# An adaLN attention block on one core: the output projection, residual and first norm of the last 512 tokens rearranged

## The chip, the core and the metric

The kernel runs on one core of a Trainium2 chip. The metric is the device time of one execution in microseconds (us); three runs of the kernel before gave 826.66, 824.58 and 827.45, median 826.66. The engines are TensorE (PE, with its weight loads as PEld), VectorE (DVE), ScalarE (ACT), GpSimd (POOL) and SyncE (SP), which issues most DMAs. Matrix products go to PSUM, eight banks of 128 x 512 float32; DVE and ACT read them there, POOL does not.

## What is computed

One transformer block with conditioning, for 2048 tokens of 512 features, 32 heads of 16, and a hidden layer of 1376:

```python
mod = (silu(c) @ w_mod).reshape(1, 6, 1, 512)      # sa, ca, ga, sb, cb, gb
h = layernorm(x) * (1 + ca) + sa
q, k, v = heads(h @ wqkv)
x = x + ga * (softmax(q @ k.T * 16 ** -0.5) @ v) @ wo
h = layernorm(x) * (1 + cb) + sb
x = x + gb * (gelu(h @ w1 + b1) @ w2 + b2)
```

## The kernel before

**Attention.** The 2048 queries are 4 blocks of 512 tokens, the 32 heads 8 groups of 4. A block and a group make a "quad"; there are 32 quads, each with 16 key tiles of 128. For a quad, PE computes the scores of 4 heads (row-tiled products, L941), and either ACT takes their exponential (L993, three or two rows at a time: `pA`, `pB`) or, for up to four key tiles of a quad, DVE makes it with integer operations (L1059, L1080: the "D" tiles). PE then adds the products with the values into one PSUM bank, `od` (L1136). An extra column of ones gives the sum of the weights in the same bank. When a quad is complete, DVE copies `od` to `o_sb` (L1168), the sums travel by DMA through DRAM and back (L1171, L1172, L1185, L1187, L1189), and POOL divides (L1193, tile `OT`). Only the last quad does this on the spot: shuffle, reciprocal and product on DVE from `o_sb` (L1177 to L1179).

**The tails.** When the 8 quads of a block are done, its tail follows: output projection (8 products for each 128 tokens), the gate `ga` (DVE, L584), the residual (POOL, L587), the statistics of the norm (DVE, L196), norm, transposes, modulation, the up projection with GELU, the down projection (L643, L645), gate `gb` and residual (L651, L655). The tails of blocks 0 to 2 run in between the attention of the next block.

**What sets the order.** A planner in the kernel's Python (`pe_step`, `dve_step`, ... and the list `jobs`) keeps a clock for each engine with costs such as `MM = 0.215` or `V_EVAC = 0.63`, and writes out each engine's instructions in the order in which its clocks allow them. A job has a due time in quads (`p0 + 0.5` is half a quad after the block's last), a list of rows (engine, cost, function), labels that it needs, and, where it needs PSUM, one of two banks `aux`, which it shares with the D tiles. `hold` tells after which row the bank is free again. Where PE has too little to do, the planner adds products with zeros (L1157). The engines themselves work strictly in the order that was written.

**The last tail** is not planned. When the last quad is complete, the pools of the attention are closed (`att.close()`), and `last_tail` writes its instructions one after the other: a pool of 8 PSUM banks `fb` on the space of the closed pools; 32 products of the output projection, quad by quad over four token tiles (L687); `norm_half(0)` for the first two token tiles: gate (L694), residual (L696), statistics on DVE; eight small operations for mean and root; the norm (L227); the eight transposes of the half (L232), read out by DVE (L272) and ACT (L269), each into a bank of its own; `norm_half(1)` with the residual on POOL (L699); the up projection of each half (L719) with GELU on ACT (L721), the down projection of four token tiles (L726, L728), gate and residual on DVE (L731, L733) and the store (L734). Between the halves' up projections stand the transposes of the second half; `range_flag` checks the sums (L753 to L761, L744, L745) for a general path that is not taken here.

Of the kernel before, what the change touches and what calls it, by code (L numbers as in the profile page):

```python
# [11 lines left out]
ALU = mybir.AluOpType  # L12
# [43 lines left out]
PE_LAT = 0.18  # L56
EXP = {1: 0.5, 2: 0.92, 3: 1.34}

EARLY = 0.95
# [28 lines left out]
def adaln_block(ctx: ExitStack, tc: tile.TileContext, A_x, A_wqkv, A_wo, B_x, B_w1, B_b1, B_w2, B_b2,  # L88
# [320 lines left out]
    def job(at, rows, needs=(), label=None, hold=-1):  # L409
        jobs.append(Job(at, rows, needs, label, hold))  # L410
# [87 lines left out]

    job(4.5, [(DVE_, 2.2, load_wo)], (), "wo")

# [55 lines left out]
    def tail_jobs(b):  # L556
# [15 lines left out]
        def oproj(tt):  # L572
            def f(part):
                def g(j):
                    if part == 0:
                        j.ps = j.alloc()
                    for t in (2 * part, 2 * part + 1):
                        nc.tensor.matmul(out=j.ps, lhsT=OT[(b, t)][:, tt * P:(tt + 1) * P], rhs=W_o_pad[:, t, :],  # L578
                                         start=(t == 0), stop=(t == 7))
                return g  # L580

            def mul(j):
                j.tmp = late["tl2"].tile([P, D], FP32, name="tmp")
                nc.vector.tensor_tensor(out=j.tmp, in0=j.ps, in1=ga_b, op=ALU.mult)  # L584

            def res(j):
                nc.gpsimd.tensor_tensor(out=T["x1"][:, tt, :], in0=j.tmp, in1=T["xr"][:, tt, :], op=ALU.add)  # L587

            def stats(j):
                ln_stats(T["x1"], T["st"], tt, tt)  # L590
            job(p0 + 0.5 + 0.25 * tt, [(PE_, 2 * MM, f(i)) for i in range(4)]
                + [(DVE_, V_EVAC, mul), (POOL_, 1.2, res), (DVE_, V_EVAC, stats)],
                ["wo", ("begin", b)] + [("ot", b, t) for t in range(8)] + ([("o", b, tt - 2)] if tt > 1 else []),
                ("o", b, tt), 4)
# [69 lines left out]
    for b in range(NQB - 1):  # L664
        tail_jobs(b)
    jobs.sort(key=lambda o: o.at)

    def last_tail():
# [3 lines left out]
        W_1, W_2, b1c = late["W_1"], late["W_2"], late["b1c"]  # L672
        xr = tl.tile([P, 4, D], BF16, name="xr")
        nc.sync.dma_start(out=xr, in_=x_tok[b])
        x1 = xr
        h2 = tl.tile([P, NC, 512], BF16, name="h2T")
# [3 lines left out]
        st = tl.tile([P, 4, 6], FP32, name="st2")  # L680
        with tc.tile_pool(name="fps", bufs=8, space=PSUM) as fps:
            def bank(dt=FP32, n=512):
                return fps.tile([P, n], dt, name="fb")
            po = [bank() for _ in range(4)]
            for t in range(8):
                for tt in range(4):
                    nc.tensor.matmul(out=po[tt], lhsT=OT[(b, t)][:, tt * P:(tt + 1) * P], rhs=W_o_pad[:, t, :],  # L687
                                     start=(t == 0), stop=(t == 7))
            def norm_half(hf):
                tts = (2 * hf, 2 * hf + 1)  # L690
                tmps = []
                for tt in tts:
                    tmp = tl2.tile([P, D], FP32, name="tmp")
                    nc.vector.tensor_tensor(out=tmp, in0=po[tt], in1=ga_b, op=ALU.mult)  # L694
                    if hf == 0:
                        nc.vector.tensor_tensor(out=x1[:, tt, :], in0=tmp, in1=xr[:, tt, :], op=ALU.add)  # L696
                        ln_stats(x1, st, tt, tt)
                    else:
                        nc.gpsimd.tensor_tensor(out=x1[:, tt, :], in0=tmp, in1=xr[:, tt, :], op=ALU.add)  # L699
                if hf:  # L700
                    for tt in tts:
                        ln_stats(x1, st, tt, tt)
# [20 lines left out]

            def down_tile(tt):
                ps = bank()
                nc.tensor.matmul(out=ps, lhsT=ones_row, rhs=late["b2r"], start=True, stop=False)  # L726
                for fc in range(NFC):
                    nc.tensor.matmul(out=ps, lhsT=uG[:, fc, tt * P:(tt + 1) * P], rhs=W_2[:, fc, :],  # L728
                                     start=False, stop=(fc == NFC - 1))
                tmp = tl2.tile([P, D], FP32, name="tmp")  # L730
                nc.vector.tensor_tensor(out=tmp, in0=ps, in1=gb_b, op=ALU.mult)  # L731
                o = tl2.tile([P, D], BF16, name="ob")
                nc.vector.tensor_tensor(out=o, in0=tmp, in1=x1[:, tt, :], op=ALU.add)  # L733
                nc.sync.dma_start(out=out_tok[4 * b + tt], in_=o)  # L734
# [40 lines left out]
    def general_tile(g, gp):  # L775
        W_1, W_2, b1c = late["W_1"], late["W_2"], late["b1c"]
        tok = bass.ds(g * P, P)
        with tc.tile_pool(name="gw", bufs=1) as gw, tc.tile_pool(name="gs", bufs=1, space=PSUM) as gs, \
# [54 lines left out]
            tmp = gw.tile([P, D], FP32, name="gtmp")  # L833
            nc.vector.tensor_tensor(out=tmp, in0=ps, in1=ga_b, op=ALU.mult)
            nc.vector.tensor_tensor(out=x1[:, 0, :], in0=tmp, in1=x1[:, 0, :], op=ALU.add)
            st = gw.tile([P, 1, 6], FP32, name="gst")
# [327 lines left out]
    def do_out(qi):  # L1164

        b, t = quads[qi]
        o = odp.tile([P, 512], FP32, name="o_sb")
        nc.vector.tensor_copy(out=o, in_=od[qi])  # L1168
# [4 lines left out]
        if qi == nq - 1:  # L1173
            rb = odp.tile([P, 512], FP32, name="rb")
            ot = otp.tile([P, 512], BF16, name="OT")
            OT[(b, t)] = ot
            nc.vector.stream_shuffle(out=rb, in_=o, mask=[16] * 32)  # L1177
            nc.vector.reciprocal(out=rb, in_=rb)
            nc.vector.tensor_tensor(out=ot, in0=o, in1=rb, op=ALU.mult)  # L1179
            return  # L1180
# [175 lines left out]
    while pv["q"] < nq or od_copy or jobs or active:  # L1356
        q = next_quad[0] - 1
        act_prog[0] = max(0.0, next_quad[0] - (len(stream) + len(unit["next"] or ())) / (4.0 * (NKT - len(d_of(q)))))
        moved = False
# [7 lines left out]
    att.close()  # L1367
    last_tail()
    general_path()

# [34 lines left out]
```

## Time and profile before

| what | value |
|---|---|
| the profiled execution's own time | 827.04 us |
| its span | 825.3 us |
| the three runs shown | 824.58 to 827.45 us, median 826.66 |
| busy share of the span | PE 94%, ACT 91%, DVE 89%, POOL 9% |
| last product of the attention issued | at about 779.1 us of the span |
| last output product ended | at about 819.9 us |
| last DVE operation ended | at about 821.3 us |
| ACT idle ahead of its exponentials, all quads | 10.3 + 11.3 us |
| filling products (L1157) | 920 into `od`, 32 into `aux` |

The profile is one execution on the chip. Times are microseconds from the start of the span; a timeline line gives start, duration (of a group of equal instructions, the whole stretch), engine, line of the kernel, operation, written and read tiles, shapes and count, and in brackets how long the engine stood idle ahead of it and what ended that. Products are pipelined: one of 128 x 512 shows 0.38 to 0.39 us, but the next follows after 0.216 us. PEclk is the share of the full clock that TensorE was granted.

### The profile page before, as it was taken

What the parts mean: (1) busy time and instruction counts of PE and PEld (TensorE: products, weight loads), DVE (VectorE), ACT (ScalarE), POOL (GpSimd) and SP (SyncE); (2) the same over time, 40 slices, a digit from 0 to 9 for tenths busy, and PEclk for the clock granted to TensorE, in tenths of its full rate; (3) what the DMA queues carried; (4) which work ended last, traced back from release to release, by engine and by line L of the source; (5) the groups of instructions that cost most, each with busy time, mean ns of one, the idle gap of its engine ahead of it and who ended that gap; (6) DMA issues with size and microseconds to landing.
All of it is one profiled execution on the core that took longest, in us unless ns stands there. A gap on an engine that the chain in (4) does not pass through costs nothing.

```text
span 825.3 us, 18246 instructions
## 1 busy us (share of the span) xinstructions
PE 774.9 (94%) x7438; PEld 239.6 (29%) x7503; DVE 732.9 (89%) x1323; ACT 750.4 (91%) x670; POOL 75.2 (9%) x68
## 2 busy tenths in 40 slices
PE   7999999999999999999999999998999999999967
PEld 3332222223222222222223222222223222222343
DVE  6858999999999899989989999989988999988573
ACT  2899799999999999999989999999999999999732
POOL 0000010010011000011021000011012000111010
PEclk8999999999999999999999999999999999999979
DMA  9000000104100000000100000100100000010000
GB/s 306 27 1 15 7 24 23 23 23 142 41 16 14 15 16 15 22 15 23 41 14 17 15 16 15 22 13 22 41 16 15 16 16 12 12 28 22 20 22 28
DMA packets 29626, 24.49 MB, mean 30 GB/s; under 512 B 13825, under 2 KB 23394, under 8 KB 29538
## 3 DMA queue, kind: packets, MB, share of 16 engines
q1 hardware_dynamic: 28482, 22.23, 9.6%
q8 instruction: 60, 0.98, 0.5%
q10 hardware_dynamic: 1056, 1.05, 0.4%
q14 instruction: 28, 0.23, 0.1%
HBM read 20.65 MB, written 2.61 MB: 28 GB/s over the span
## 4 chain that ended last, share of the span: by engine, by line
PE 42%; ACT 30%; DVE 16%; issue 10%; DMA 2%; SPq 0%; POOL 0%; ACTq 0%; DVEq 0%; POOLq 0%
ACT pA L993 16%; PE od L1136 12%; ACT pB L993 11%; DVE t L1059 6%; PE sA L941 6%; DVE t L1080 5%; PE sB L941 5%; PE aux L645 3%; PE aux L941 3%; PE aux L578 2%; ACT uG L634 2%; PE fb L719 1%; PE od L1157 1%; PE aux L620 1%; PE fb L728 1%
## 5 line engine op out<-in xcount | busy, mean ns | idle before, releaser
L993 ACT ACTIVATE pA<-sA 128x1536 bf16<-128x1536 f32 x310 | 469.3, 1514 | 10.3 <-PE od L1136 5.4
L1059 DVE TENSOR_SCALAR t<-aux 128x512 int16<-128x512 f32 x500 | 327.8, 679 | 29.2 <-PE aux L941 27.5
L993 ACT ACTIVATE pB<-sB 128x1024 bf16<-128x1024 f32 x309 | 337.0, 1091 | 11.3 <-PE od L1136 6.1
L1080 DVE TENSOR_SCALAR t<-t 128x2048 int16<-128x2048 int16 x375 | 262.8, 722 | 2.1 <-PE od L1136 0.5
L941 PE MATMUL aux<-qm,kT 32*128 32x512 bf16 x500 | 176.3, 379 | 3.3 <-DVE t L1059 1.6
L941 PEld LDWEIGHTS <-kT 32*128 32x128 bf16 x2048 | 77.6, 91 | 268.6 <-issue 263.7
L1136 PE MATMUL od<-pA,VE 128*32 128x512 bf16 x930 | 143.5, 385 | 0.4 <-DVE o_sb L1168 0.4
L1136 PE MATMUL od<-pB,VE 128*32 128x512 bf16 x618 | 142.5, 385 | 0.0
L1136 PE MATMUL od<-t,VV 128*32 128x512 f16 x1500 | 137.8, 384 | 1.6 <-DVE t L1080 1.5
L941 PE MATMUL sA<-qm,kT 32*128 32x512 bf16 x930 | 123.2, 383 | 14.4 <-ACT pA L993 9.6
L941 PE MATMUL sB<-qm,kT 32*128 32x512 bf16 x618 | 121.2, 383 | 5.8 <-ACT pB L993 2.1
L1193 POOL TENSOR_TENSOR OT<-o_sb,rb 128x512 bf16<-128x512 f32 x31 | 41.6, 1342 | 530.0 <-DMA rb<-d 363.2
L1157 PE MATMUL od<-hT,zeros 128*32 128x512 bf16 x920 | 80.8, 383 | 0.0
L1136 PEld LDWEIGHTS <-VE 128*32 128x32 bf16 x2048 | 50.1, 94 | 99.3 <-issue 86.5
L1136 PEld LDWEIGHTS <-VV 128*32 128x32 bf16 x1500 | 40.0, 95 | 55.9 <-issue 46.5
L1136 PE MATMUL od<-t,VE 128*32 128x512 f16 x500 | 49.2, 384 | 0.9 <-DVE o_sb L1168 0.9
L620 PE MATMUL aux<-h2T,W 128*128 128x512 bf16 x114 | 36.0, 385 | 0.8 <-DVE t L1059 0.7
L645 PE MATMUL aux<-W,uG 128*128 128x512 bf16 x119 | 34.9, 383 | 1.8 <-issue 1.7
L1157 PEld LDWEIGHTS <-zeros 128*32 128x32 bf16 x952 | 23.3, 95 | 36.4 <-issue 29.2
L1168 DVE COPY o_sb<-od 128x512 f32<-128x512 f32 x32 | 21.8, 682 | 8.7 <-issue 8.5
L625 DVE TENSOR_SCALAR uG<-aux,b1c 128x512 bf16<-128x512 f32 x33 | 24.3, 737 | 2.7 <-PE aux L620 2.6
L578 PE MATMUL aux<-W_o_pad,OT 128*128 128x512 bf16 x88 | 24.7, 383 | 0.3 <-issue 0.3
(129 smaller groups left out, 418.4 us busy)
## 6 DMA issues: line engine op xcount, KB each, us to landing
rb<-d SPq DMA_DIRECT2D x124, 64.0 KB
W_m<-in_w_mod_dram SPq DMA_DIRECT2D x2, 1024.0 KB
xr<-in_A_x_dram SPq DMA_DIRECT2D x4, 512.0 KB
out_dram<-ob SPq DMA_DIRECT2D x16, 128.0 KB
xb<-in_A_x_dram SPq DMA_DIRECT2D x3, 512.0 KB
W<-in_B_w_dram SPq DMA_DIRECT2D x1, 1376.0 KB
W<-in_B_w_dram SPq DMA_DIRECT2D x1, 1280.0 KB
W_m<-in_w_mod_dram ACTq DMA_DIRECT2D x1, 1024.0 KB
```

What stands on the lines that cost most here:

```text
L578: nc.tensor.matmul(out=j.ps, lhsT=OT[(b, t)][:, tt * P:(tt + 1) * P], rhs=W_o_pad[:, t, :], start=(t == 0), stop=(t == 7))
L620: nc.tensor.matmul(out=j.ps, lhsT=late["W_1"][:, c, fc * P:(fc + 1) * P], rhs=T["h2"][:, c, :], start=(c == 0), stop=(c == NC - 1))
L625: nc.vector.tensor_scalar(out=T["u"][:, fc, :], in0=j.ps, scalar1=late["b1c"][:, fc:fc + 1], scalar2=None, op0=ALU.add)
L645: nc.tensor.matmul(out=j.ps, lhsT=T["u"][:, fc, tt * P:(tt + 1) * P], rhs=late["W_2"][:, fc, :], start=False, stop=(fc == NFC - 1))
L941: nc.tensor.matmul(out=dst, lhsT=kT[32 * r:32 * r + 32, ch, kt * P:(kt + 1) * P], rhs=qm[(b, ch)][32 * r:32 * r + 32, par, :], start=True, ...
L993: nc.scalar.activation(out=pt[:, 0:n, :], in_=st[:, 0:n, :], func=ACT.Exp, scale=math.log(2.0) / STEP)
L1059: nc.vector.tensor_scalar(out=t0[(qi, kt)][:, r, :], in0=sd, scalar1=T_BIAS, scalar2=0.0, op0=ALU.add, op1=ALU.max)
L1080: nc.vector.tensor_scalar(out=t16, in0=t0[(qi, kt)], scalar1=float(MJ[j]), scalar2=None, op0=ALU.add)
L1136: nc.tensor.matmul(out=od[qi][32 * r:32 * r + 32, :], lhsT=w, rhs=src, start=first, stop=last_)
L1157: nc.tensor.matmul(out=dst[32 * r:32 * r + 32, :], lhsT=zeros, rhs=hT[:, r, 0:512], start=bank is not None, stop=bank is not None)
L1168: nc.vector.tensor_copy(out=o, in_=od[qi])
L1193: nc.gpsimd.tensor_tensor(out=OT[(b, t)], in0=o, in1=j.rb, op=ALU.mult)
```

## The change

The gate `ga` is multiplied once into the output weights (`scale_wo`: eight POOL products of 128 x 512, planned at quads 6 to 7.4). The residual comes into PSUM as one more product, of the identity with the tokens `xr`, ahead of the eight of each token tile; in the tails of blocks 0 to 2 a DVE copy then takes the place of gate and POOL residual. The due times of the down projection's four tiles are 0.6 quads apart, formerly 0.5.

For the last block, the load of its tokens (`last_begin`) and the projections of token tiles 0 and 1 without the last quad's part are planned jobs in the last quad, in the two `aux` banks, which now belong to a pool that stays open. `last_tail` has six PSUM banks on the space of the attention's closed pools. It writes the seven quads' products of tiles 2 and 3, five products that are not used (`keep_on`), the last quad's four products, and eighteen more unused ones. The statistics are read from PSUM by DVE, the sums copied to SBUF by ACT. A one-column GELU stands ahead of the first transposes. Two transposed chunks share one PSUM bank. The down projection of tile 0 stands ahead of the second half's transposes, and that of tile 3 is done in two halves of 256 columns. The last quad's shuffle and product read `od` itself, and the copy `o_sb` comes after them.

```diff
+KEEP = (5, 18)
...
+    def scale_wo(t):
+        nc.gpsimd.tensor_tensor(out=W_o_pad[:, t, :], in0=W_o_pad[:, t, :], in1=ga_b, op=ALU.mult)
...
+    bk = ExitStack()
+    banks = [bk.enter_context(tc.tile_pool(name=f"psX{i}", bufs=1, space=PSUM)) for i in range(2)]
     att = ExitStack()
...
-    banks = [att.enter_context(tc.tile_pool(name=f"psX{i}", bufs=1, space=PSUM)) for i in range(2)]
...
-    job(4.5, [(DVE_, 2.2, load_wo)], (), "wo")
+    job(4.5, [(DVE_, 2.2, load_wo)], (), "wo_in")
+    for t in range(8):
+        job(6.0 + 0.2 * t, [(POOL_, 1.2, lambda j, t=t: scale_wo(t))], ["wo_in", "ga"], ("wo", t))
...
+                        nc.tensor.matmul(out=j.ps, lhsT=ident, rhs=T["xr"][:, tt, :], start=True, stop=False)
...
-            def mul(j):
-                j.tmp = late["tl2"].tile([P, D], FP32, name="tmp")
-                nc.vector.tensor_tensor(out=j.tmp, in0=j.ps, in1=ga_b, op=ALU.mult)
-
             def res(j):
-                nc.gpsimd.tensor_tensor(out=T["x1"][:, tt, :], in0=j.tmp, in1=T["xr"][:, tt, :], op=ALU.add)
+                nc.vector.tensor_copy(out=T["x1"][:, tt, :], in_=j.ps)
...
-            job(p0 + 4.9 + 0.5 * tt, [(PE_, (3 if i == 0 else 1 if i == 5 else 2) * MM, f(i)) for i in range(6)]
+            job(p0 + 4.9 + 0.6 * tt, [(PE_, (3 if i == 0 else 1 if i == 5 else 2) * MM, f(i)) for i in range(6)]
...
+    def last_begin(j):
+        last["xr"] = late["tl"].tile([P, 4, D], BF16, name="xr")
+        nc.sync.dma_start(out=last["xr"], in_=x_tok[NQB - 1])
+
+    job(8 * NQB - 1.2, [(SP_, 3.0, last_begin)], [("tail", NQB - 2)], "last")
+
+    def o_mm(ps, tt, t):
+
+        if t == 0:
+            nc.tensor.matmul(out=ps, lhsT=ident, rhs=last["xr"][:, tt, :], start=True, stop=False)
+        nc.tensor.matmul(out=ps, lhsT=OT[(NQB - 1, t)][:, tt * P:(tt + 1) * P], rhs=W_o_pad[:, t, :],
+                         start=False, stop=(t == 7))
+
+    def last_oproj(tt):
...
+        job(8 * NQB - 1.0 + 0.05 * tt, [(PE_, n * MM, f(i)) for i, n in enumerate((3, 2, 2, 1))],
+            ["last", "d_done"] + [("ot", NQB - 1, t) for t in range(7)], ("last", tt), 99)
...
-        with tc.tile_pool(name="fps", bufs=8, space=PSUM) as fps:
+        with tc.tile_pool(name="fps", bufs=6, space=PSUM) as fps:
...
-            po = [bank() for _ in range(4)]
-            for t in range(8):
-                for tt in range(4):
-                    nc.tensor.matmul(out=po[tt], lhsT=OT[(b, t)][:, tt * P:(tt + 1) * P], rhs=W_o_pad[:, t, :],
-                                     start=(t == 0), stop=(t == 7))
+            po = [last[0], last[1], bank(), bank()]
+            for tt in (2, 3):
+                for t in range(7):
+                    o_mm(po[tt], tt, t)
+
+
+            idle = bank()
+
+            def keep_on(n):
+                for _ in range(n):
+                    nc.tensor.matmul(out=idle, lhsT=ident, rhs=hT[:, 0, 0:512], start=True, stop=True)
+            keep_on(KEEP[0])
+            for tt in range(4):
+                o_mm(po[tt], tt, 7)
+            keep_on(KEEP[1])
...
+                    nc.vector.bn_stats(out=st[:, tt, :], in_=po[tt])
+                    nc.scalar.copy(out=x1[:, tt, :], in_=po[tt])
...
-                    pst = bank(BF16, 256)
+                    if j % 2 == 0:
+                        two = bank(BF16, 512)
+                    pst = two[:, 256 * (j % 2):256 * (j % 2) + 256]
...
             norm_half(0)
+
+            early = tl.tile([P, 1], FP32, name="early")
+            nc.scalar.activation(out=early, in_=b1c[:, 0:1], func=ACT.Gelu_apprx_tanh)
             transposes(0)
             norm_half(1)
             up_half(0)
+            down_tile(0)
             transposes(1)
             up_half(1)
...
-            for tt in range(4):
+            for tt in (1, 2):
                 down_tile(tt)
+            down_tile(3, 2)
...
+        if qi == nq - 1:
+            rb = odp.tile([P, 512], FP32, name="rb")
+            nc.vector.stream_shuffle(out=rb, in_=od[qi], mask=[16] * 32)
+            nc.vector.reciprocal(out=rb, in_=rb)
+            ot = otp.tile([P, 512], BF16, name="OT")
+            OT[(b, t)] = ot
+            nc.vector.tensor_tensor(out=ot, in0=od[qi], in1=rb, op=ALU.mult)
         o = odp.tile([P, 512], FP32, name="o_sb")
         nc.vector.tensor_copy(out=o, in_=od[qi])
...
         if qi == nq - 1:
-            rb = odp.tile([P, 512], FP32, name="rb")
-            ot = otp.tile([P, 512], BF16, name="OT")
-            OT[(b, t)] = ot
-            nc.vector.stream_shuffle(out=rb, in_=o, mask=[16] * 32)
-            nc.vector.reciprocal(out=rb, in_=rb)
-            nc.vector.tensor_tensor(out=ot, in0=o, in1=rb, op=ALU.mult)
             return
```

More of the change, by code (lines that the diff above doesn't have):

```diff
@@ L576, in g @@
                         j.ps = j.alloc()
+                        nc.tensor.matmul(out=j.ps, lhsT=ident, rhs=T["xr"][:, tt, :], start=True, stop=False)
                     for t in (2 * part, 2 * part + 1):
                         nc.tensor.matmul(out=j.ps, lhsT=OT[(b, t)][:, tt * P:(tt + 1) * P], rhs=W_o_pad[:, t, :],
-                                         start=(t == 0), stop=(t == 7))
+                                         start=False, stop=(t == 7))
                 return g
-            def mul(j):
-                j.tmp = late["tl2"].tile([P, D], FP32, name="tmp")
-                nc.vector.tensor_tensor(out=j.tmp, in0=j.ps, in1=ga_b, op=ALU.mult)
             def res(j):
-                nc.gpsimd.tensor_tensor(out=T["x1"][:, tt, :], in0=j.tmp, in1=T["xr"][:, tt, :], op=ALU.add)
+                nc.vector.tensor_copy(out=T["x1"][:, tt, :], in_=j.ps)
             def stats(j):
                 ln_stats(T["x1"], T["st"], tt, tt)
-            job(p0 + 0.5 + 0.25 * tt, [(PE_, 2 * MM, f(i)) for i in range(4)]
-                + [(DVE_, V_EVAC, mul), (POOL_, 1.2, res), (DVE_, V_EVAC, stats)],
-                ["wo", ("begin", b)] + [("ot", b, t) for t in range(8)] + ([("o", b, tt - 2)] if tt > 1 else []),
+            job(p0 + 0.5 + 0.25 * tt, [(PE_, (2 + (i == 0)) * MM, f(i)) for i in range(4)]
+                + [(DVE_, V_EVAC, res), (DVE_, V_EVAC, stats)],
+                [("begin", b)] + [("wo", t) for t in range(8)] + [("ot", b, t) for t in range(8)] + ([("o", b, tt - 2)] if tt > 1 else []),
                 ("o", b, tt), 4)
@@ L665, in adaln_block, with f, g @@
         tail_jobs(b)
+    last = {}
+    def last_begin(j):
[6 more added lines that the diff above has]
+        nc.tensor.matmul(out=ps, lhsT=OT[(NQB - 1, t)][:, tt * P:(tt + 1) * P], rhs=W_o_pad[:, t, :],
+                         start=False, stop=(t == 7))
+    def last_oproj(tt):
+        def f(part):
+            def g(j):
+                if part == 0:
+                    j.ps = last[tt] = j.alloc()
+                for t in range(2 * part, min(7, 2 * part + 2)):
+                    o_mm(j.ps, tt, t)
+            return g
+        job(8 * NQB - 1.0 + 0.05 * tt, [(PE_, n * MM, f(i)) for i, n in enumerate((3, 2, 2, 1))],
+            ["last", "d_done"] + [("ot", NQB - 1, t) for t in range(7)], ("last", tt), 99)
+    for tt in range(2):
+        last_oproj(tt)
     jobs.sort(key=lambda o: o.at)
@@ L672, in last_tail @@
         W_1, W_2, b1c = late["W_1"], late["W_2"], late["b1c"]
-        xr = tl.tile([P, 4, D], BF16, name="xr")
-        nc.sync.dma_start(out=xr, in_=x_tok[b])
-        x1 = xr
+        x1 = last["xr"]
         h2 = tl.tile([P, NC, 512], BF16, name="h2T")
@@ L680, in last_tail @@
         st = tl.tile([P, 4, 6], FP32, name="st2")
-        with tc.tile_pool(name="fps", bufs=8, space=PSUM) as fps:
+        with tc.tile_pool(name="fps", bufs=6, space=PSUM) as fps:
             def bank(dt=FP32, n=512):
                 return fps.tile([P, n], dt, name="fb")
-            po = [bank() for _ in range(4)]
-            for t in range(8):
-                for tt in range(4):
-                    nc.tensor.matmul(out=po[tt], lhsT=OT[(b, t)][:, tt * P:(tt + 1) * P], rhs=W_o_pad[:, t, :],
-                                     start=(t == 0), stop=(t == 7))
+            po = [last[0], last[1], bank(), bank()]
[10 more added lines that the diff above has]
+            keep_on(KEEP[1])
             def norm_half(hf):
                 tts = (2 * hf, 2 * hf + 1)
-                tmps = []
                 for tt in tts:
[L693 to L702, printed above, removed]
+                    nc.vector.bn_stats(out=st[:, tt, :], in_=po[tt])
+                    nc.scalar.copy(out=x1[:, tt, :], in_=po[tt])
                 mv, rs = ln_rstd(st[:, 2 * hf:2 * hf + 2, :], 2)
@@ L722, in up_half, with down_tile @@
                                          bias=b1c[:, fc:fc + 1], scale=1.0)
[L724 to L729, printed above, removed]
-                tmp = tl2.tile([P, D], FP32, name="tmp")
[L731 to L734, printed above, removed]
+            def down_tile(tt, parts=1):
+                o = tl2.tile([P, D], BF16, name="ob")
+                tmp = tl2.tile([P, D], FP32, name="tmp")
+                n = D // parts
+                for c in range(parts):
+                    cs = slice(c * n, c * n + n)
+                    ps = bank(FP32, n)
+                    nc.tensor.matmul(out=ps, lhsT=ones_row, rhs=late["b2r"][:, cs], start=True, stop=False)
+                    for fc in range(NFC):
+                        nc.tensor.matmul(out=ps, lhsT=uG[:, fc, tt * P:(tt + 1) * P], rhs=W_2[:, fc, cs],
+                                         start=False, stop=(fc == NFC - 1))
+                    nc.vector.tensor_tensor(out=tmp[:, cs], in0=ps, in1=gb_b[:, cs], op=ALU.mult)
+                    nc.vector.tensor_tensor(out=o[:, cs], in0=tmp[:, cs], in1=x1[:, tt, cs], op=ALU.add)
+                    nc.sync.dma_start(out=out_tok[4 * b + tt][:, cs], in_=o[:, cs])
             norm_half(0)
+            early = tl.tile([P, 1], FP32, name="early")
+            nc.scalar.activation(out=early, in_=b1c[:, 0:1], func=ACT.Gelu_apprx_tanh)
             transposes(0)
@@ L833, in general_tile @@
             tmp = gw.tile([P, D], FP32, name="gtmp")
-            nc.vector.tensor_tensor(out=tmp, in0=ps, in1=ga_b, op=ALU.mult)
-            nc.vector.tensor_tensor(out=x1[:, 0, :], in0=tmp, in1=x1[:, 0, :], op=ALU.add)
+            nc.vector.tensor_tensor(out=x1[:, 0, :], in0=ps, in1=x1[:, 0, :], op=ALU.add)
             st = gw.tile([P, 1, 6], FP32, name="gst")
@@ L1357, in adaln_block @@
         q = next_quad[0] - 1
+        if not d_tiles and not d_items:
+            lab.setdefault("d_done", clock)
         act_prog[0] = max(0.0, next_quad[0] - (len(stream) + len(unit["next"] or ())) / (4.0 * (NKT - len(d_of(q)))))
@@ L1368, in adaln_block @@
     last_tail()
+    bk.close()
     general_path()
```

## Prediction

> **What bounds the kernel now.** I read the page's busy shares first (PE 94%, ACT 91%, DVE 89%), then the groups by line, the waits, and the timeline from 777 us. Up to 779 us PE and ACT keep each other at work; ACT waits ahead of its exponentials only 10.3 + 11.3 us in all:
>
> ```profile
> L993 ACT ACTIVATE pA<-sA 128x1536 bf16<-128x1536 f32 x310 | 469.3, 1514 | 10.3 <-PE od L1136 5.4
> L993 ACT ACTIVATE pB<-sB 128x1024 bf16<-128x1024 f32 x309 | 337.0, 1091 | 11.3 <-PE od L1136 6.1
> DVE st L196 <- POOL xr L587: 3.6, 4, 1.3
> ```
>
> The third line (waits) is all that the residual on POOL costs DVE. After 779 us a chain alternates between DVE and PE (timeline: start, duration, engine, line, tiles, in brackets the idle time before and what ended it):
>
> ```profile
> 779.56 0.69 DVE L1168 COPY o_sb<-od 128x512 f32<-128x512 f32 x1 [8.55 <-issue]
> 780.30 0.72 DVE L1177 STREAM_SHUFFLE rb<-o_sb 128x512 f32<-128x512 f32 x1
> 780.40 7.07 PE L687 MATMUL fb<-W_o_pad,OT 128*128 128x512 bf16 x31 [0.72 <-DVE o_sb L1168]
> 781.05 3.35 DVE L1178 RECIPROCAL rb<-rb 128x512 f32<-128x512 f32 x1
> 784.44 0.69 DVE L1179 TENSOR_TENSOR OT<-o_sb,rb 128x512 bf16<-128x512 f32 x1
> 786.93 0.69 DVE L694 TENSOR_TENSOR tmp<-fb,ga_b 128x512 f32<-128x512 f32 x1 [1.79 <-PE fb L687]
> 793.20 0.73 DVE L227 TENSOR_SCALAR hnL<-xr,mv,rs 128x512 bf16<-128x512 bf16 x2
> 793.67 1.25 PE L232 MATMUL fb<-ident,hnL 128*128 128x128 bf16 x8 [6.20 <-DVE hnL L227]
> ```
>
> Two things are to be seen. PE stands idle for 6.2 us before the transposes. And the first output product waits for the copy `o_sb`, though it reads nothing of it: the new pool lies on the space of the closed ones and waits for their last reader. The rows of windows (length, busy PE, PEld, DVE, ACT, POOL, granted clock) show the price of the idle time:
>
> ```profile
> 787.00:788.00 1.00, 0.47 (x3) 0.00 (x0) 0.91 (x2) 0.00 (x0) 0.00 (x0) 1.00 0.00 0
> 789.00:790.00 1.00, 0.00 (x0) 0.00 (x0) 0.97 (x3) 0.00 (x0) 0.00 (x0) 0.87 0.00 0
> 790.00:791.00 1.00, 0.00 (x0) 0.00 (x0) 0.97 (x2) 0.00 (x0) 0.00 (x0) 0.50 0.00 0
> 799.00:800.00 1.00, 1.00 (x7) 0.71 (x5) 0.83 (x6) 0.57 (x2) 0.00 (x0) 0.51 0.00 0
> 800.00:801.00 1.00, 1.00 (x11) 0.89 (x10) 0.82 (x6) 0.77 (x2) 0.00 (x0) 1.00 0.00 0
> ```
>
> PE stopped at 787.47, the clock fell at about 789.7 and came back at 800.0, 6.3 us after work began again at 793.67. Both steps are 10.3 us apart.
>
> **Quads 0 to 30.** Removed: 12 gate products and 12 POOL sums; added: 12 copies (0.68 each, from `o_sb`'s group), 12 identity products (12 x 0.216 = 2.6 us of PE) and 8 POOL products of some 1.3 us in quads 6 and 7, where POOL has 90% free; if they came late, the first output projection, in quad 8, would wait. The changed program's order has 900 filling products where before had 952, so most of the 2.6 us replaces filling. At best the 3.6 us of DVE's wait and part of ACT's idle time go; at worst 12 + 16 products add 28 x 0.216 = 6 us less 52 fillings of about 0.065 (16 in 1.04 us), 3.4: about +2.6. I take -0.7, near the gain's lower half, since DVE seldom ends ACT's waits; the range keeps -3.6 to +2.6. The token load goes from SP's free stretch at 782 us to just after the sums of quad 30 go out, ahead of the store of their reciprocals (764.4). That quad's `OT` was ready at 772.3 (POOL, 770.99 + 1.27) and would be wanted by the planned products near 776: 3.7 us of slack, beyond which PE's scores queue behind them. The two planned projections sit in the two `aux` banks after the last D tile. Cost nothing while that slack holds.
>
> **The wait that moves.** In the changed program's order the copy `o_sb` is last of DVE's four operations, and PE's first product of tile 2 (7 + identity, then tile 3) still waits for it. So the chain is: shuffle 779.56, reciprocal 780.31, product 783.70 (each 0.74 earlier, the copy being gone), copy 784.42 to 785.11, PE at 785.26 (0.15 after the copy, as before). PE is idle 779.47 to 785.26, 5.8 us. The planned start would have been near 779.5: the 16 products that were to fill this gap stand behind it.
>
> First statistics: 16 + 5 products x 0.2155 = 4.53, start of the last quad's first at 789.79, 0.50 until DVE can read (before: product 28 x 0.2155 after 780.40, DVE at 786.93): 790.29 warm. After an idle time of 5.8 us the clock is low: the idle stretch of before sufficed after 2.3 us. Low for 3.4 to 6.8 us of work (6.3 in the row above, and half of that at best if a step falls well), half of it lost: 1.7 to 3.4; I take 2.4. So 792.65, against 786.93. From there the old chain to `hnL` took 6.27; four of its operations (2 gate, 2 residual, 2.85 by the starts) are gone: 3.42, `hnL` 796.07. Three forms have no row yet: shuffle, product and statistics that read PSUM. Their rows from SBUF are 0.72, 0.69 and 0.69, DVE's copy and gate from PSUM take 0.69 each, so I take them as unchanged; at twice the statistics' price it would be 1.4 more, at none 1.4 less. The sums' copies by ACT (0.55 for 256 columns, 1.09 for 1024, so some 0.7) wait for the statistics of their tile in the same bank and end near 794.7, ahead of `hnL`: hidden, and beyond 796.07 each microsecond would count. PE is held by the 18 products: 785.26 + 43 x 0.2155 + 2.4 = 796.93, transposes there instead of 793.67: **+3.26**.
>
> [...]
>
> **Transposes.** Two chunks share a bank, so each second chunk's transposes wait for the reading of the first, and DVE and ACT alternate. By the rows below (0.41 each on DVE, 0.55 on ACT, 0.3 to 0.4 from PE to reader) full rate comes 2.55 after the first transpose, where it was 1.98: up projection at 799.5 against 795.65, **+3.85**. The table load (1.28) goes into ACT's idle time before the transposes, where it costs nothing; it did not bind before either.
>
> ```profile
> 794.32 0.83 DVE L272 TENSOR_SCALAR h2T<-fb,modc 128x256 bf16<-128x256 bf16 x2 [0.39 <-PE fb L232]
> 794.58 1.02 ACT L269 ACTIVATE h2T<-fb,modc 128x256 bf16<-128x256 bf16 x2 [15.57 <-PE fb L232]
> ...
> 796.09 1.28 ACT L721 ACT_TABLE_LOAD   x1 [0.49 <-issue]
> ...
> 802.53 1.37 DVE L272 TENSOR_SCALAR h2T<-fb,modc 128x256 bf16<-128x256 bf16 x4 [0.88 <-PE fb L232]
> ...
> 804.26 4.84 ACT L721 ACTIVATE uG<-fb,b1c 128x256 bf16<-128x256 f32 x11 [1.37 <-PE fb L719]
> 819.91 0.69 DVE L731 TENSOR_TENSOR tmp<-fb,gb_b 128x512 f32<-128x512 f32 x1 [1.38 <-PE fb L728]
> 820.63 0.69 DVE L733 TENSOR_TENSOR ob<-tmp,xr 128x512 bf16<-128x512 f32 x1
> ```
>
> [...]
>
> **To the end.** The up projection now runs warm: 39 remaining products x 0.113 to 803.85 (before half cold, to 802.38). The down projection of tile 0 (2.80, the pitch of four) follows to 806.65; GELU (11 in 4.84) is done by 805.4. Then the second half's transposes, but DVE first has tile 0's gate and residual (1.41), and the read-outs alternate with PE through shared banks: full rate 1.41 + 2.3 later, 810.35, against 803.95: +6.4, of which 2.8 is the tile moved ahead. Up 4.64, flag 0.09, three tiles of 2.80: PE ends at 823.6, against 819.87. Then 5.43 to the end of the span as before, less 0.54 for the last gate and sum at half width (0.41 against 0.69): 828.45 against 825.3: **+3.15**.
>
> In 806.65 to 810.35 PE has some 1.0 us of work in 3.7. Stretches of one clock step with 34% and with 36 to 50% busy let the clock fall; one with 65% did not. So a second low stretch is likely, by my estimate at 2 in 3: half of 3.4 to 6.8 us less what falls into the stall: 0 to 2.6; I take **+2.0**.
>
> Sum on the profiled 827.04 (span 825.3 + 1.74): +3.15 + 2.0 - 0.7 = 831.5. The median of the runs is 0.38 lower: **831.1**.
>
> **Rivals.** A, as worked out: 828 to 836, chance 0.58. B: no second low stretch, and the attention gains 3 us from POOL's absence: 826.66 + 3.15 - 3 = 826.8. For it speaks ACT's idle 21.6 us; against it, that PE ends most of these waits. 0.24. C, faster: tile 2's first product does not wait for the copy, and starts before the shuffle ends (780.3). Then PE never cools, statistics come at about 785, transposes at 789.2, up at 791.8, the second half 802.75, PE's end 816.0 and the span's 820.85: 822.2. It decides by that one start; for it speaks only that the product needs neither `od` nor `o_sb`, against it the row of 780.40. 0.12. D: `OT` of quad 30 late by the load on SP, PE held 3 us: 834. 0.06.
>
> 0.3%, 2.5 us, is about what a measurement of this kernel can tell from no change: 824.2 to 829.1. Slower: A but 0.03, D, and 0.02 of B, 0.63 rounded to 0.64; same 0.24; faster 0.12, C. The range of 8 in 10 leaves out C and the ends of A and D: 825 to 836.
>
> **What would show it.** Right: the first residual product of tile 2 at about 785, its idle time ended by `o_sb`; clock at 0.5 there; statistics near 792.6; transposes near 797; between up projections a PE gap of 3 to 4 us with the clock at half after it. Wrong: a start near 779.5 (C), a full clock throughout (B), exponentials ending more than 3 us from 779, or POOL's last `OT` after 776 (D).

## The result, and the profile after it

The changed kernel takes 831.02 us (median of 13 runs, 829.01 to 836.21), the kernel before 827.38 (13 runs beside them, 824.58 to 830.52): ratio 1.0052, interval 1.0037 to 1.0068. The forecast was 831.1 on a before of 826.66, 4.4 more; measured are 3.6 more between the medians and 4.3 by the ratio. The profiled execution of the changed kernel takes 830.93 with a span of 829.2.

The chain behind the last attention product, from the changed kernel's timeline (columns as in the prediction):

```profile
777.74 0.72 DVE L1212 STREAM_SHUFFLE rb<-od 128x512 f32<-128x512 f32 x1
778.50 3.35 DVE L1213 RECIPROCAL rb<-rb 128x512 f32<-128x512 f32 x1
781.89 0.69 DVE L1216 TENSOR_TENSOR OT<-od,rb 128x512 bf16<-128x512 f32 x1
782.50 0.68 DVE L1218 COPY o_sb<-od 128x512 f32<-128x512 f32 x1
783.24 0.61 PE L682 MATMUL fb<-xr,ident 128*128 128x512 bf16 x1 [5.64 <-DVE o_sb L1218]
790.82 1.30 DVE L735 BATCH_NORM_STATS2 st<-aux 128x6 f32<-128x512 f32 x2 [7.64 <-PE aux L683]
794.20 0.74 DVE L229 TENSOR_SCALAR hnL<-xr,mv,rs 128x512 bf16<-128x512 bf16 x2
795.15 0.28 PE L234 MATMUL fb<-ident,hnL 128*128 128x128 bf16 x2
```

The bracket of L682 is the line to find. PE stood idle 5.64 us and was released by the copy, which neither the identity nor the tokens nor bank `fb` needs. The windows of one microsecond (clock third from the right) show what the idle time set off, there and a second time between the halves:

```profile
781.00:782.00 1.00, 0.00 (x0) 0.00 (x0) 0.97 (x2) 0.00 (x0) 0.00 (x0) 0.87 0.00 0
788.00:789.00 1.00, 1.00 (x5) 0.40 (x4) 0.00 (x0) 0.00 (x0) 0.00 (x0) 0.71 0.00 0
809.00:810.00 1.00, 1.00 (x7) 0.73 (x6) 0.93 (x3) 0.49 (x2) 0.00 (x0) 0.53 0.00 0
812.00:813.00 1.00, 1.00 (x9) 0.79 (x8) 0.00 (x0) 0.62 (x2) 0.00 (x0) 0.77 0.00 0
```

With the clock at 1 or 0.5 (1.00 in the window 789:790, 0.50 in 782:783), a mean of 0.87 puts the fall at 781.74, and 0.71 the rise at 788.58: low for 6.8 us. The second low stretch runs from about 809.1 to 812.5, 3.4 us. What lies ahead of it, in the timeline:

```profile
805.21 0.69 DVE L771 TENSOR_TENSOR tmp<-fb,gb_b 128x512 f32<-128x512 f32 x1 [4.41 <-PE fb L769]
805.93 0.69 DVE L772 TENSOR_TENSOR ob<-tmp,xr 128x512 bf16<-128x512 f32 x1
806.54 0.41 DVE L274 TENSOR_SCALAR h2T<-fb,modc 128x256 bf16<-128x256 bf16 x1
808.87 6.30 PE L755 MATMUL fb<-h2T,W 128*128 128x256 bf16 x41 [0.17 <-DVE h2T L274]
```

PE had the first transposes at 805.01, but DVE did tile 0's gate and residual first and read the transposes only at 806.54. The 41 products then take 6.30 us; at the full clock, in the first half, they took 4.64.

In one number: from DVE's first operation after the last attention product to DVE's last of all, before took 41.76 us (779.56 to 821.32), the changed kernel 47.07 (777.74 to 824.81). I call this stretch the tail. The attention ended 1.8 earlier in the changed kernel of this pair of profiles, what follows DVE's last operation took 4.4 instead of 4.0, and 5.3 - 1.8 + 0.4 is the 3.9 between the spans. The 1.8 are hardly the change's: they stand already at the copy of quad 4 (154.12 against 155.92), ahead of the gate's first product at 171.75. Before's profile has the clock at half from 11.5 to 18.3 us, the changed kernel's has not, and from that copy to the tail both take 623.6.

### The profile page after: what moved, and what is told of

Read it like the earlier page. It is cut to its first block, busy times and chain, and to the rows that moved or that the text cites. A ratio compares the mean times of both kernels' runs of the same rounds, so it can differ in the third digit from the quotient of the medians.

```text
span 829.2 us, 18300 instructions
## 1 busy us (share of the span) xinstructions
PE 785.1 (95%) x7502; PEld 239.4 (29%) x7502; DVE 728.0 (88%) x1319; ACT 752.7 (91%) x675; POOL 70.9 (9%) x62
## 3 DMA queue, kind: packets, MB, share of 16 engines
HBM read 20.65 MB, written 2.61 MB: 28 GB/s over the span
## 4 chain that ended last, share of the span: by engine, by line
PE 45%; ACT 25%; DVE 19%; issue 9%; DMA 1%; SPq 0%; POOL 0%; ACTq 0%; DVEq 0%; POOLq 0%
PE od L1179 13%; ACT pA L1036 13%; ACT pB L1036 10%; DVE t L1102 7%; PE sA L984 6%; DVE t L1123 6%; PE sB L984 5%; PE aux L984 3%; PE aux L650 3%; PE aux L587 3%; PE od L1200 2%; PE aux L625 2%; PE fb L755 1%; PE fb L769 1%; ACT uG L639 1%
## 5 line engine op out<-in xcount | busy, mean ns | idle before, releaser
L1102 DVE TENSOR_SCALAR t<-aux 128x512 int16<-128x512 f32 x500 | 329.1, 682 | 34.1 <-PE aux L984 33.3
L1123 DVE TENSOR_SCALAR t<-t 128x2048 int16<-128x2048 int16 x375 | 262.0, 723 | 2.0 <-PE od L1179 0.8
L984 PE MATMUL aux<-qm,kT 32*128 32x512 bf16 x500 | 179.6, 380 | 4.0 <-DVE t L1102 3.2
L1200 PE MATMUL od<-hT,zeros 128*32 128x512 bf16 x880 | 78.1, 384 | 0.0
L625 PE MATMUL aux<-h2T,W 128*128 128x512 bf16 x132 | 39.6, 384 | 0.3 <-DVE t L1102 0.3
L650 PE MATMUL aux<-W,uG 128*128 128x512 bf16 x132 | 38.9, 384 | 0.0
L587 PE MATMUL aux<-W_o_pad,OT 128*128 128x512 bf16 x96 | 27.9, 382 | 0.0
L660 POOL TENSOR_TENSOR ob<-tmp,xr 128x512 bf16<-128x512 f32 x12 | 15.3, 1271 | 116.6 <-DVE tmp L656 116.6
```

The lines of the kernel that those rows point to most:

```text
L625: nc.tensor.matmul(out=j.ps, lhsT=late["W_1"][:, c, fc * P:(fc + 1) * P], rhs=T["h2"][:, c, :], start=(c == 0), stop=(c == NC - 1))
L984: nc.tensor.matmul(out=dst, lhsT=kT[32 * r:32 * r + 32, ch, kt * P:(kt + 1) * P], rhs=qm[(b, ch)][32 * r:32 * r + 32, par, :], start=True, ...
L1102: nc.vector.tensor_scalar(out=t0[(qi, kt)][:, r, :], in0=sd, scalar1=T_BIAS, scalar2=0.0, op0=ALU.add, op1=ALU.max)
L1123: nc.vector.tensor_scalar(out=t16, in0=t0[(qi, kt)], scalar1=float(MJ[j]), scalar2=None, op0=ALU.add)
L1200: nc.tensor.matmul(out=dst[32 * r:32 * r + 32, :], lhsT=zeros, rhs=hT[:, r, 0:512], start=bank is not None, stop=bank is not None)
```

## Experiments

Theory 1: the loss is the wait that moved. A product of the new pool waits for the last reader of any tile on the space of the closed pools; the copy was the first of four DVE operations and is now the last. Theory 2: the unused products, the shared banks and tile 0 ahead of the transposes make the loss. Theory 3: the attention lost. The times of each run stand beside runs of before on the same chip (medians from 826.66 to 827.52); ratios are against those, and differences between versions that were measured on different chips are given by both medians and ratios where they differ much.

**The copy first again.**

```diff
-        if qi == nq - 1:
-            rb = odp.tile([P, 512], FP32, name="rb")
-            nc.vector.stream_shuffle(out=rb, in_=od[qi], mask=[16] * 32)
...
-            nc.vector.tensor_tensor(out=ot, in0=od[qi], in1=rb, op=ALU.mult)
         nc.vector.tensor_copy(out=o, in_=od[qi])
...
         if qi == nq - 1:
+            rb = odp.tile([P, 512], FP32, name="rb")
...
+            nc.vector.stream_shuffle(out=rb, in_=o, mask=[16] * 32)
+            nc.vector.reciprocal(out=rb, in_=rb)
+            nc.vector.tensor_tensor(out=ot, in0=o, in1=rb, op=ALU.mult)
             return
```

> Changed kernel with one edit: the copy o_sb again ahead of shuffle, reciprocal and product, which read o_sb as before the change. Theory 1 (the wait that moved: PE's first product of tile 2 waits for the copy, and the clock falls in the gap): PE starts tile 2 some 0.15 us after the copy, the 16 products lie beside the reciprocal, PE's idle time there falls from 5.6 us to under 1.5, the clock stays full, the last quad's products start some 7 us earlier relative to the last attention product; time about 824 against 831. Rival 2 (the 18 unused products, shared banks and the second stall make the loss): no more than 1 us gained, 830. Rival 3 (the loss lies in the attention, from the gating on POOL): 830 to 831.

824.95, ratio 0.9971 (0.9954 to 0.9988). Tail 38.39, clock full throughout. Its timeline:

```profile
777.20 0.69 DVE L1211 COPY o_sb<-od 128x512 f32<-128x512 f32 x1 [9.48 <-issue]
777.95 0.38 PE L682 MATMUL fb<-xr,ident 128*128 128x512 bf16 x1 [0.85 <-DVE o_sb L1211]
```

Idle time 0.85 instead of 5.64, still ended by the copy. 6.1 us between the medians, 6.7 by the ratios, go with the order of one operation: theory 1.

**od in a pool of its own**, opened ahead of the scores' pools in the stack that stays open.

```diff
-    psO = att.enter_context(tc.tile_pool(name="psO", bufs=1, space=PSUM))
+    psO = bk.enter_context(tc.tile_pool(name="psO", bufs=1, space=PSUM))
...
-        with tc.tile_pool(name="fps", bufs=6, space=PSUM) as fps:
+        with tc.tile_pool(name="fps", bufs=5, space=PSUM) as fps:
...
-                        two = bank(BF16, 512)
+                        two = psO.tile([P, 512], BF16, name="od") if j == 0 else bank(BF16, 512)
```

> Changed kernel with one edit: od's bank stays in a pool that is not closed, and the tail's pool (5 banks) lies on the score banks alone; the copy stays last. If the wait comes from the space of the closed pools and not from data (theory 1), PE goes on with tile 2 at once after the last attention product, without idle time, although the copy is still last; last quad's products start about 0.7 us earlier than in the run with the copy first; time about 823.3. If the wait was for something else that the copy stands for (a rival to the mechanism), PE still starts at the copy's end and the time is 831. Rivals 2 and 3: 830 to 831.

823.43, ratio 0.9943 (0.9925 to 0.9962). Here the copy is the last operation, as in the changed kernel, and its timeline reads:

```profile
779.63 0.39 PE L682 MATMUL fb<-xr,ident 128*128 128x512 bf16 x1
...
784.60 0.68 DVE L1218 COPY o_sb<-od 128x512 f32<-128x512 f32 x1
```

PE goes on without idle time, five microseconds ahead of the copy. So the wait was one for space, not for data. The statistics come 5.36 after the start of the tail, 0.69 earlier than with the copy first (6.05); tail 39.05, with a second low stretch of 3.4 us that the profile before this one does not have.

**The other way round: before, with the copy last.** Only shuffle and product from `od` and the copy behind them, in the kernel before.

> The kernel before with this one part of the change: shuffle and product read od, and the copy o_sb comes after them. Theory (the first product on the new pool waits for the copy wherever it stands): PE is idle 5.7 us, the output projection starts 5.6 us after the last attention product instead of 0.9, 28 of its products lie on the path, 4.9 us later and 1.7 to 3.4 more at the low clock; from the last attention product to DVE's last operation 48 to 50 us instead of 41.8, time about 834. Rival (the product waits only for the last quad's OT, which comes 0.7 us earlier): 826.5.

834.16, ratio 1.0084 (1.0067 to 1.0101), tail 48.44. Its timeline:

```profile
784.90 0.68 DVE L1175 COPY o_sb<-od 128x512 f32<-128x512 f32 x1
785.73 9.16 PE L687 MATMUL fb<-W_o_pad,OT 128*128 128x512 bf16 x32 [5.50 <-DVE o_sb L1175]
```

This one part of the change costs 7.0 us alone, more than the whole change. The version with its own pool, which has the rest of the change without the wait, is 4.1 faster than before: the rest gives some of the loss back.

**Tile 0's down projection back behind the second up projection** (`down_tile(0)` taken out ahead of `transposes(1)`, `for tt in (0, 1, 2)` at the end).

> Changed kernel with one edit: the down projection of tile 0 again behind the second half's up projection. Theory (DVE's gate and residual of that tile stand ahead of the read-outs, and the stall lets the clock fall a second time): the gap between the up projections falls from 3.9 to about 2.4 us, the second low stretch goes (the profile of the changed kernel has 3.4 us of it, so 1.7 us); time about 831.0 - 1.4 - 1.7 = 828. If only the gap shrinks and the clock still falls: 829.6. Rival (tile 0 ahead costs nothing, since it fills PE while DVE normalises): 831 or more, with a wait of PE for hnL instead.

**DVE's part of tile 0 later, PE's order kept**: `down_tile` writes its products and puts gate, residual and store into `later`.

```diff
-            down_tile(0)
+            later = []
+            down_tile(0, 1, later)
             transposes(1)
+            for r in later:
+                r()
```

> Changed kernel with one edit: DVE's gate and residual of tile 0 are written after the second half's read-outs; PE's order stays (down projection of tile 0 ahead of the transposes). Theory (the stall between the up projections is DVE's order, not PE's): gap from the first transpose of the second half to the full rate 2.4 instead of 3.9 us, low clock there mostly gone, time 828 to 829, as with the tile put back. Rival (PE's order makes it): 831.

828.70, ratio 1.0025 (1.0006 to 1.0044, which still overlaps the changed kernel's interval), and 827.93, ratio 1.0017 (1.0004 to 1.0031, which does not). Neither profile has a second low stretch, and from the start of `hnL` to the end of the tail both take 27.73 us, the changed kernel 30.61. PE's order makes no difference. DVE's two operations of 0.69 ahead of the read-outs were 1.2 of the stall's 3.9 (802.61 to 805.25 is left in the second run), and the second low stretch went with them: of the 2.9 us, 1.66 were the clock (6.30 against 4.64). That part also depends on chance, since two of six profiles with the stall of 3.9 have no low stretch either. My rival of PE's order fell.

**A bank for each transposed chunk** (`pst = bank(BF16, 256)` for each `j`).

> Changed kernel with one edit: each transposed chunk has its own bank again. Theory (shared banks make PE's transposes wait for each read-out): first transpose to the up projection at full rate 1.9 instead of 2.6 us in the first half, 0.6 less in the second; 829.8. If the second stall then also no longer lets the clock fall: 828. Rival (the read-outs by DVE and ACT bound it anyway): 831 within 0.5.

828.71, ratio 1.0009 (0.9995 to 1.0023). PE in the first half, in the changed kernel (some rows left out) and then in this run:

```profile
795.15 0.28 PE L234 MATMUL fb<-ident,hnL 128*128 128x128 bf16 x2
795.93 0.38 PE L234 MATMUL fb<-ident,hnL 128*128 128x128 bf16 x4 [0.50 <-DVE h2T L274]
796.92 0.49 PE L755 MATMUL fb<-h2T,W 128*128 128x256 bf16 x3
```

```profile
795.91 0.61 PE L234 MATMUL fb<-ident,hnL 128*128 128x128 bf16 x8
796.69 5.42 PE L753 MATMUL fb<-h2T,W 128*128 128x256 bf16 x44 [0.17 <-DVE h2T L274]
```

From the first transpose to the start of the later products that is 0.8 us instead of 1.8; from `hnL` to the end 27.00. No second low stretch either, though DVE's two operations still stood ahead: the stall had shrunk from 3.9 to 2.0. The read-outs by DVE and ACT follow closer where the banks differ: in the version with all parts, further down, ACT's first starts 0.11 us after DVE's first (787.54 against 787.43), in the changed kernel 0.82 (796.28 against 795.46).

**The gate on one column only.**

```diff
-        nc.gpsimd.tensor_tensor(out=W_o_pad[:, t, :], in0=W_o_pad[:, t, :], in1=ga_b, op=ALU.mult)
+        nc.gpsimd.tensor_tensor(out=W_o_pad[:, t, 0:1], in0=W_o_pad[:, t, 0:1], in1=ga_b[:, 0:1], op=ALU.mult)
```

> Changed kernel, but the gate is multiplied into one column of the output weights only (the rest of the gate is left out, so the output is not the reference's); order and products are the same, POOL's eight products last some 0.1 instead of 1.3 us. Theory (POOL's products on the weights hold up DVE's integer operations in quads 6 and 7: 128 x 2048 takes 1.65 instead of 0.68 us beside them, PE waits and its clock falls): quads 5 to 7 take 40.7 us as in before instead of 42.3 to 45.0 in the changed kernel's profiles, the clock stays full there, time about 828 against 831. Rival (what is lost there is given back by the fills and waits later): 830.5 to 831.

827.63, ratio 1.0014 (0.9999 to 1.0028). The run was prompted by a stretch of the changed kernel's profile. DVE, then POOL:

```profile
195.73 2.61 DVE L1123 TENSOR_SCALAR t<-t 128x2048 int16<-128x2048 int16 x2
198.27 1.27 DVE L1102 TENSOR_SCALAR t<-aux 128x512 int16<-128x512 f32 x2
199.47 1.68 DVE L1123 TENSOR_SCALAR t<-t 128x2048 int16<-128x2048 int16 x1
```

```profile
195.06 2.74 POOL L381 TENSOR_TENSOR W_o_pad<-W_o_pad,ga_b 128x512 bf16<-128x512 bf16 x2
199.33 1.27 POOL L1237 TENSOR_TENSOR OT<-o_sb,rb 128x512 bf16<-128x512 f32 x1 [1.53 <-DMA rb<-d]
200.55 4.30 POOL L381 TENSOR_TENSOR W_o_pad<-W_o_pad,ga_b 128x512 bf16<-128x512 bf16 x3
```

Two operations on 128 x 2048 int16 take 1.04 and 1.65 us beside the gate's products (2.61 from the first's start to the second's end), and one takes 1.68 beside the division `OT` and the product after it. The division is not new: beside it the operation takes up to 1.78 in before as well (at 677.47; 1.43 in quads 4 to 7, at 214.41). The run with the gate on one column has, ahead of its division (which starts at 200.51):

```profile
197.00 1.28 DVE L1123 TENSOR_SCALAR t<-t 128x2048 int16<-128x2048 int16 x2
199.40 0.69 DVE L1123 TENSOR_SCALAR t<-t 128x2048 int16<-128x2048 int16 x1
```

L1102, which reads PSUM, keeps 0.67 to 0.69 in both. Added up between the copies `o_sb` of quads 4 and 7, what the operations on 128 x 2048 take beyond 0.70 us each is 5.6 us in the changed kernel, 1.5 in before and 1.1 here. The price shows between the same two copies: before 65.24 us; eight profiles with the long POOL products 67.3 to 70.1, mean 68.6, five of them with a low clock there, which none of the six profiles without these products has; the gate on one column 64.86. So the eight products cost some 3.4 to 3.7 us, and the time of the kernel, 3.4 less (3.1 by the ratios), says the same.

**The gate in pieces of 128 columns.**

```diff
-        nc.gpsimd.tensor_tensor(out=W_o_pad[:, t, :], in0=W_o_pad[:, t, :], in1=ga_b, op=ALU.mult)
+        for c in range(0, D, 128):
+            nc.gpsimd.tensor_tensor(out=W_o_pad[:, t, c:c + 128], in0=W_o_pad[:, t, c:c + 128],
+                                    in1=ga_b[:, c:c + 128], op=ALU.mult)
```

> Changed kernel with one edit: POOL multiplies the gate in pieces of 128 columns, 32 short products instead of 8 long ones. Theory (a DVE operation on 128 x 2048 int16 cannot start or go on while a POOL product runs, and waits for that product's end): such an operation takes at most 1.1 instead of up to 1.8 us, the clock stays full in quads 6 and 7, half to all of the 3.4 us come back that the run without the gate showed: 828 to 829.5. Rival (the two engines share bandwidth in proportion, so that the length of a piece makes no difference): 831, with DVE's operations as long in the mean as before.

829.95, ratio 1.0028 (1.0009 to 1.0048). In the profile the DVE operation takes 0.87 in the median between 195 and 205 us and at most 0.92, the clock stays full there, and quads 4 to 7 take 65.81 us, near the 64.86 without the gate. Beyond its 0.70 the operation loses 3.1 us in all there instead of 5.6, so the rival, by which the mean stays, falls. A wait for the end of the running product fits: one operation loses at most 1.0 us beside the changed kernel's products of 1.16 to 1.61, and at most 0.26 (0.94 in all) beside pieces of 0.43 to 0.88. POOL itself pays for it: the 32 pieces take 18.2 us in all, the eight products 10.6. And the time of the kernel fell by 1.1 to 2 us only and its interval overlaps that of the changed kernel: how much of the 3.4 the pieces bring back in all runs stays open.

**Without the products that keep PE at work**, on the version with its own pool (`KEEP = (0, 0)`).

> The version with od's bank in its own pool (823.4), without the 5 and the 18 unused products. Theory (idle time of over 2 us costs a clock step, so the products that keep TensorE at work are worth something once the wait is gone): PE idle 1.6 us ahead of the last quad's products and 3.9 us ahead of the transposes, clock at half in the first up projection, 1.7 to 3.4 us lost: 825 to 827. Rival (the unused products only hold up the transposes): 823.0 to 823.4.

824.45, ratio 0.9992 (0.9970 to 1.0014), against 0.9943 with them. PE was idle 1.49 us ahead of the last quad's products, with no fall of the clock, and 3.35 ahead of the transposes:

```profile
785.64 0.48 PE L234 MATMUL od<-ident,hnL 128*128 128x128 bf16 x2 [3.35 <-DVE hnL L229]
```

The clock was low from 785.96 to 792.78, and the first up projection took 7.48 us for its 44 products, from 787.88 on, instead of 5.5 (791.28 to 796.77). The 2 us of the theory are an estimate: these rows show only that 1.49 of idle time gave no fall and 3.35 did. The unused products are worth 1 us by the medians and 4 by the ratios, once PE can start in time. By this profile the 18 do that; that the 5 do anything no run shows. As to the rival, the 18 do hold up the transposes, but only by some 0.4 us: they start 0.93 after the start of `hnL` with them and 0.56 without.

**The attention's part alone**: weights, identity products, copies and due times in the kernel before, its own last tail kept.

> The kernel before with the change's part in quads 0 to 30 alone: gated weights, identity products, DVE copies, down projections 0.6 apart; the last tail as before, with a copy in place of its gate (0.69 either way). Prediction: -0.7 against before, 826.3 on a before of 827.0. Theory after the profiles: a gain of about 1 to 2 net, some 4 gained by the plan and by POOL's absence, some 2.5 lost by POOL's products on the weights: 825.5 to 826.5. Rival: the attention lost, and the five profiles show luck: 828.

825.98, ratio 0.9991 (0.9973 to 1.0008); tail 41.73, as before. The sign can't be told from this, and my -0.7 stands within it. But the sum hides two terms: quads 4 to 7 take 70.07 us in its profile (before 65.24), and from the copy of quad 7 to the end of the attention 553.1 (before 558.4). The second term is 553 to 556 in all profiles of the new order, and 558.8 in that of before with the copy last, whose attention is the old one.

**Together**: own pool; banks of od, the two `aux` and one of the tail for the four chunks; DVE's part of tile 0 later; the gate in pieces.

> What the runs point to, together: od in its own pool, a bank for each transposed chunk (od's, the two aux banks, one of the tail's pool), DVE's gate and residual of tile 0 after the read-outs, POOL's gate in pieces. If the parts add up: from the last attention product to DVE's last operation 34.5 us (41.8 in before, 47.1 in the changed kernel, 39.0 with the own pool alone), no low clock in the tail, time about 818 against 827 of before. Rival (the parts share one gain, since the low clock stretches are the same): 821.

819.32, ratio 0.9906 (0.9879 to 0.9933), tail 34.44 where 34.5 was expected, the clock full in the whole tail. So the parts add up in the tail. The time is 1.3 us above the 818, and 1.7 below the rival's 821.

**And the second half's transposes inside the first up projection**, after 8 of 11 blocks, tile 0 last again.

> The same, with the second half's transposes inside the first half's up projection, after 8 of its 11 blocks, and the down projection of tile 0 last again. Theory (the read-outs then lie beside 1.4 us of PE's work): the gap between the up projections nearly goes, 1.2 to 1.4 us less than the version with all parts: about 816.5. Rival (the second half's norm is not ready after 8 blocks, and PE waits in the middle instead): 818 or more.

817.21, ratio 0.9878 (0.9849 to 0.9908): the fastest, by 9.5 us between the medians and 10.1 by the ratio, where the changed kernel lost 3.6. But the tail became 33.91, only 0.5 shorter, and the theory's 1.2 to 1.4 fell: in the version before it the gap from the second half's first transpose to its first product was only 0.78 us (795.88 to 796.66), most of it the transposes themselves, and here it is 0.73 (792.02 to 792.75). Separate banks and DVE's order had closed it already. The 2.1 between the medians are therefore mostly not the transposes'; the intervals of the two versions overlap.

## Why the prediction was right, step by step

**The wait that moves** was the main step, and each of its terms held, but for two slips that hardly count: the four starts of gates and residuals give 2.94 and not 2.85, and 790.29 + 2.4 is 792.69. From the start of the tail, predicted and measured: PE's idle time 5.8 and 5.64; first statistics 13.1 and 13.08; `hnL` 16.5 and 16.46; first transposes 17.4 and 17.41; first up projection at full rate 19.9 and 20.0. The low clock cost 2.7 (5.3 us of work from 783.24 to 788.58, half lost), where I took 2.4 out of 1.7 to 3.4. The 3.4 to 6.8 us of work behind that range were my estimate: the row beside it shows 6.3, and half of that is 3.15. The traces have low stretches of 6.82 (11.50 to 18.32) and 10.24 us (789.74 to 799.98) in before, and here one of 6.84, of which 5.3 lie after the restart. Statistics and shuffle from PSUM cost what they cost from SBUF (0.69 each in the mean, L735 and before's L196; 0.72, L1212 and before's L1177).

**To the end**: second half at full rate 30.8 and 31.1; PE's end 46.0 (with the second low stretch) and 46.2. PE's end is worked out 0.1 too late in the prediction: 810.35 + 4.64 + 0.09 + 3 x 2.80 is 823.5. The second low stretch came, 1.66 for 2.0. Six profiles have the same stall of 3.9 and four of them the low stretch (changed kernel, own pool, gate on one column, pieces; not the copy first, nor the run without unused products), so the chance of 2 in 3 was fair, and that it came in the profile shown is in part luck. The sign that I had chosen, PE's busy share in one step of the clock (3.41 us, half of before's 6.82), does sort them: 0.29 to 0.34 in the step ahead of the fall in the four, 0.51 and 0.61 in the emptiest step of the two. As a rule it does not hold: a step with 0.49 kept the clock (run without unused products, from 779.13), one with 0.62 lost it (changed kernel, from 198.07).

**Half-width last tile**: mis-sized. I gave 0.54. PE's last product ended at 823.90, the span at 829.2, so 5.3 us follow where before had 5.43: 0.1. DVE's part did shrink by the 0.54 (1.45 to 0.91 after PE's end), but what follows DVE's last operation grew from 4.0 to 4.4; it is 3.9 to 4.1 in the three profiles with the old end of the tail and 4.2 to 4.8 in all others.

**Quads 0 to 30**: the sum was right, -0.7 against -1.0 (825.98 against 826.96; -0.7 by the ratio; not told from zero). From the copy of quad 4 to the tail the eight profiles with the long products take 622.8 in the mean, the two of the old attention 623.6 and 623.9. The step "8 POOL products of some 1.3 us in quads 6 and 7, where POOL has 90% free" failed: I looked at whether POOL had time, not at what its work does to DVE. It cost some 3.5. The gain behind it was larger than I allowed, some 4 us in quads 8 to 31 by the profiles (mean 554.6 against 558.4 and 558.8); whether from POOL's 12 sums that no longer stand beside DVE, or from the other order that the planner wrote after quad 8, no run separated. The profiles hint at both: from the copy of quad 7 to that of quad 31 the operations on 128 x 2048 lose 10.5 us beyond 0.70 each in before and 5.3 to 8.0 in the new order, but only 1.7 of the 10.5 lie beside the sums, most of the others beside the divisions. Two errors cancelled, so that this sum came out right is luck.

What POOL's products did to DVE differs by operation: the one from SBUF to SBUF (L1123) went from 0.69 to 1.65 us beside the long products, and to at most 0.94 beside the pieces, while L1102, from PSUM, stayed at 0.67 to 0.69. Why the two differ no run separated.

**Rivals.** C was decided as written, by the start of tile 2's first product: 783.24, not ahead of the shuffle's end at 778.46. Its price was near: the version that makes its condition true takes 823.43 where 822.2 was worked out. B's gain in the attention did come in quads 8 to 31, 4 us for the 3 it took, but POOL's products on the weights took it away again. D did not come: POOL's last `OT` ended at 770.96, some 3.1 us ahead of the product that reads it (within L683's three from 773.64 on; 3.7 was worked out).

## To carry to other kernels

When an operation is moved on one engine, look at who waits for it by its place, not by its data: here a new pool on the space of closed ones waited for their last reader (PE idle for 5.64 us), and this wait, for one copy behind three other operations, turned a gain of 4 us (own pool) into a loss of 3.6. Products that are to fill a gap cannot do so from behind the wait that makes it: here the 16 of tiles 2 and 3 and the first five unused ones all stood behind the copy. Free time on an engine was not enough to hide work on it (POOL, busy 9% of the span, took on eight products, and they cost some 3.5 us); its effect on the neighbour has to be looked up in rows where both are busy.

## What the runs showed of the hardware

The low stretches of the clock within these executions come in whole steps of about 3.4 us (3.40, 6.82 and 6.84 in the changed kernel, 6.82 and 10.24 in before, without those that the end of the span cuts short), and the same gap did not always give as many: 5.64 us gave 6.8 us in five profiles and 3.4 in one (the run with tile 0 put back, 783.18 to 786.60). What differs is where the gap lies against the steps: in that one PE began again 0.4 us after the fall, in the five others 1.5 to 3.6 us after it (1.5 in the changed kernel, 783.24 after 781.75). Idle times in the tail of 0.85 (copy first), 1.49 (without unused products) and 0.41 us (own pool) gave none. The changed program's runs spread over 829.0 to 836.2 us, and the mean granted clock of each run goes with that: 0.994 in the fastest, 0.984 in the two slowest (834.58 and 836.21), and in the version with the copy first from 0.996 at 821.76 to 0.981 at 830.66. So low stretches go with the spread; that they make all of it was not tested.

Where two chunks share a bank, PE, reader and PE follow each other (idle 0.50 us ahead of the transposes at 795.93, ended by the read-out): 1.8 us from the first transpose to the later products (795.15 to 796.92), against 0.8 with a bank for each (795.91 to 796.69).
